# Turning queries with four transposes of token pairs in a retention and gated feed-forward kernel

## The chip, the cores and the metric

The kernel runs on one core of one Trainium2 chip. The metric is device time in microseconds of one execution. A core has TensorE (PE in the profile, its weight loads PEld), VectorE (DVE), ScalarE (ACT), GpSimd (POOL) and SyncE (SP), which here issues most of the DMA transfers. Matmul results go to PSUM; everything else lives in SBUF.

## The reference

Two blocks follow each other. The first is recurrent retention over 4 batches, 8 heads, 768 tokens and 64 dimensions a head, all float32:

```python
for t in range(S):
    state = gamma * state + einsum('bhd,bhe->bhde', k[:, :, t], v[:, :, t])
    y[:, :, t] = scale * einsum('bhd,bhde->bhe', q[:, :, t], state)
```

Its output, laid out as 3072 tokens of 512 features, is `x` of the second block, a feed-forward layer with 2048 hidden features:

```python
h = x @ w_in
g = h * (1.0 / (1.0 + np.exp(-1.702 * h)))
return g @ w_out
```

The weights are handed to the kernel as 8-byte words and narrowed to float32 on the chip.

## The kernel before, in words

**Retention.** The tokens are cut into chunks of 64. A step `j` handles one chunk of two batches (all 8 heads), so there are 24 steps. For each: queries and keys are turned so that the head dimension lies on partitions (`turn`), `scores` makes keys times queries, `masked` weighs them by decay, `own` multiplies them by the values, `past` multiplies the queries by the state, `by_state` and `output` add the two into `X`, `gain`, `aged` and `updated` carry the state to the next chunk; `decay` weighs the keys for it. These are bursts of 64x64 matmuls (L327, L335, L346, L355), 64 TensorE instructions each with the loads, and PSUM tiles `pa` and `py` that they share.

**Steps 0 to 5 and the rest.** For the first six steps (`NEW = 6`) the turn is TensorE's; from step 6 on it is done by DVE (L288). For `j < NEW` one DMA brings the queries as a tile of 128 rows and 512 columns: a row is one batch, head and block of 8 tokens, and holds these 8 tokens of 64 dimensions one after another (L155). Keys come with tokens on the rows (L146). `turn_new` (L265) makes a PSUM tile `pt` with tag `y`, of which there are two, shared with other products. Keys take four transposes of 128x128 (L278). Queries take 16 matmuls against columns picked from the identity (L275), one for each of 8 tokens and each half of the heads, in float32, so that the profile counts 32 matmuls and 32 loads; each writes its result into `pt` with the tokens already at their places and with half of the heads in each half of the partitions. `turned` (L296) then copies the whole tile to `QT[j]` or `KT[j]` in SBUF: one 128x512 operation on ACT (L294).

**Weights.** Every half megabyte or so of weights is fetched by SP (`w1a` and so on, L189) into one of three raw buffers and narrowed by `abs` (ACT, L225), `low` (ACT, L229), `clip` (DVE, L233), `lift` (DVE, L236), `sign` (DVE, L241) and `rest` (DVE, L246). The first products of the feed-forward block (`up0`, L464) use a weight once its `rest` is done: `up0.0.2` needs weight 0, `up0.0.3` weight 2, `up0.0.6` weight 3, `up0.0.7` weight 1. `gate` (ACT, L445) is the activation on such a product.

**The order.** Nothing is planned for the first part: a list of names written out by hand (L1092 to L1114) is gone through once, and every name issues its instructions on its engine. Each engine, and the queue of SP, takes its own in that order. For the steps spoken of here, the list has (shortened):

```python
turned_k1 turned_q1 q2 score1 rowd whole w2b turn_k2 turn_q2
... score2 q4 x1 clip2 lift2 sign2 low2 decay3 w3b w3a up0.0.2 masked2 turn_k3 turn_q3
k4@sp gain2 past2 own2 v3 q5 rest2 k5@sp gate0.0.2 turned_k3 turned_q3 updated2 state2 score3 decay4 low3
turn_q4 turn_k4 up0.0.3 x2 masked3 gain3 past3 own3 abs3 clip3 lift3 sign3 turned_q4 rest3 turned_k4 score4
turn_k5 turn_q5 up0.0.6 ...
```

Here `q4`, `k4`, `v3` are loads, `turn_*` TensorE's part and `turned_*` the copy. Query tiles have two buffers, so that `q5` on SP waits until TensorE has turned queries 3.

**After the list.** The second part, by far the longer, consists of Strassen-like products (`up` at L686, `down49` at L809, `down` at L942) with the later retention steps set between them, and DVE makes the sums of weights and activations for them.

## Time and profile before

| what | value |
|---|---|
| median of 3 runs | 654.35 us (654.05 to 658.25) |
| the profiled execution | 654.23 us, span of its instructions 652.5 us |
| mean clock granted to TensorE | 0.99 |
| query turns (L275) | 192 matmuls of 128x64, 222 ns in the median, at 4.8 to 45.7 us |
| key turns on TensorE (L278) | 24 matmuls of 128x128, 273 ns in the median |
| copies of turned tiles (L294, G<-pt) | 12 on ACT, 594 ns in the median |

How to read what follows. A line of the timeline has the start in us from the span's start, the time from the first to the last instruction of a group, the engine, the line of the kernel, the operation, the program's names as out<-in, the shapes, a count, and in brackets the idle time of the engine before it with what ended that. "issue" stands for no visible cause. PEld are weight loads, which overlap the matmuls and show TensorE's order best; SPq and ACTq are DMA issues. On the page, a row of 40 digits shows the busy share of 40 equal slices (16.3 us each) in tenths; PEclk is the clock granted to TensorE in tenths. A matmul's own duration is its way through the array; matmuls follow each other much closer than that, so durations of a row of them are taken from start to start.

### The profile page before, as it was taken

The page shows a single profiled execution, that of the slowest core. Times are in us where ns is not written, and L with a number is a line of the kernel's source. Part 1 is how long each engine was busy: PE and PEld are TensorE (multiplying, and loading weights), DVE is VectorE, ACT ScalarE, POOL GpSimd, SP SyncE. Part 2 cuts the span into 40 slices and gives each one's busy share as a digit, 9 for nine tenths or more (in the row PEclk, how much of TensorE's full clock was granted, in tenths as well). Part 3 has the DMA queues.
Part 4 walks back from the last instruction along what each step waited for, and adds up shares of the span by engine and source line. Part 5 has one row for each costly group of instructions (what it writes and reads, how often), then busy time and mean ns, then how long its engine had stood idle before and what let it go on. Part 6 is the DMA issues. An engine that isn't in the chain of part 4 may idle for free.

```text
span 652.5 us, 15859 instructions
## 1 busy us (share of the span) xinstructions
PE 636.0 (97%) x6717; PEld 579.5 (89%) x6718; DVE 433.3 (66%) x630; ACT 187.6 (29%) x343; POOL 152.7 (23%) x183
## 2 busy tenths in 40 slices
PE   7699999999998999999999999999999999999997
PEld 3588888888888999889999889999888999888997
DVE  2559977979989774438874337977145986144854
ACT  5668237662000101332101333100323110333210
POOL 3000311310622535000635100526300425200000
PEclk7799999999999999999999999999999999999999
DMA  8968577783358778520577830576921354501143
GB/s 186 235 202 212 112 231 212 209 219 56 98 181 282 170 177 257 141 72 1 164 167 213 235 70 14 156 168 196 244 48 49 82 165 138 207 11 48 57 156 97
DMA packets 150728, 96.89 MB, mean 148 GB/s; under 512 B 130528, under 2 KB 135904, under 8 KB 149632
## 3 DMA queue, kind: packets, MB, share of 16 engines
q1 hardware_dynamic: 138032, 42.83, 29.9%
q0 software_dynamic: 8704, 40.00, 19.6%
q10 hardware_dynamic: 3920, 13.04, 5.4%
q8 instruction: 53, 0.87, 0.6%
q14 instruction: 19, 0.16, 0.1%
HBM read 79.18 MB, written 14.94 MB: 144 GB/s over the span
## 4 chain that ended last, share of the span: by engine, by line
PE 82%; DVE 7%; DMA 5%; SPq 3%; issue 2%; ACT 0%; DVEq 0%
PE pq L809 34%; PE px L686 17%; PE pz L686 8%; PE ph L587 6%; PE py L686 4%; DVE X L762 2%; PE pa L327 2%; PE pd L942 2%; SPq L164 2%; DMA kn_in<-in_k_dram 2%; PE ph L464 1%; PE py L355 1%; PE ph L547 1%; PE py L346 1%; PE pa L335 1%
## 5 line engine op out<-in xcount | busy, mean ns | idle before, releaser
L809 PE MATMUL pq<-W,G 128*128 128x128 f32 x840 | 100.3, 276 | 0.0
L809 PEld LDWEIGHTS pq<-W,G 128*128 128x128 f32 x840 | 97.0, 192 | 0.8
L784 POOL DMA_DIRECT2D LATE<-W2D x34 | 18.9, 555 | 258.3 <-PE pq L809 140.0
L809 PE MATMUL pq<-LATE 128*128 128x128 f32 x560 | 74.9, 277 | 0.7 <-DVE o L918 0.7
L809 PEld LDWEIGHTS pq<-LATE 128*128 128x128 f32 x560 | 68.1, 192 | 1.5 <-DVE o L918 0.9
L686 PE MATMUL px<-X,LATE 128*128 128x256 f32 x256 | 60.6, 380 | 0.1
L686 PE MATMUL px<-X,W1A 128*128 128x256 f32 x256 | 60.5, 379 | 0.0
L686 PEld LDWEIGHTS px<-X,LATE 128*128 128x128 f32 x256 | 48.6, 190 | 7.0 <-ACT G L445 0.4
L686 PEld LDWEIGHTS px<-X,W1A 128*128 128x128 f32 x256 | 48.4, 190 | 6.4
L831 ACT ACTIVATE o<-pq 128x512 f32<-128x512 f32 (+1 forms) x18 | 9.8, 544 | 121.4 <-PE pq L809 101.7
L731 DVE TENSOR_TENSOR G<-pz,vv 128x512 f32<-128x512 f32 x16 | 11.1, 692 | 49.4 <-ACT vv L701 49.4
L445 ACT ACTIVATE G<-G 128x512 f32<-128x512 f32 x49 | 30.8, 629 | 43.5 <-DVE G L741 19.7
L809 PE MATMUL pq<-W,LATE 128*128 128x128 f32 x280 | 37.3, 276 | 0.7 <-issue 0.7
L809 PE MATMUL pq<-LATE,G 128*128 128x128 f32 x280 | 37.0, 275 | 0.0
L942 PE MATMUL pd<-W,LATE 128*128 128x256 f32 x160 | 35.1, 380 | 0.0
L809 PEld LDWEIGHTS pq<-W,LATE 128*128 128x128 f32 x280 | 34.2, 192 | 0.8 <-issue 0.8
L809 PEld LDWEIGHTS pq<-LATE,G 128*128 128x128 f32 x280 | 34.1, 192 | 0.0
L942 PEld LDWEIGHTS pd<-W,LATE 128*128 128x128 f32 x160 | 30.4, 190 | 4.1
L464 PE MATMUL ph<-X,W1A 128*128 128x256 f32 x128 | 31.0, 401 | 0.6 <-DVE X L397 0.6
L671 DVE TENSOR_TENSOR G<-G 128x512 f32<-128x512 f32 (+2 forms) x28 | 15.9, 567 | 23.5 <-ACT G L445 23.5
L798 DVE TENSOR_TENSOR LATE<-G 128x512 f32<-128x512 f32 x35 | 27.7, 791 | 5.0 <-PE pq L809 2.1
L686 PE MATMUL pz<-X,W1A 128*128 128x256 f32 x128 | 30.3, 380 | 0.0
(212 smaller groups left out, 1168.4 us busy)
## 6 DMA issues: line engine op xcount, KB each, us to landing
LATE<-W2D POOLq DMA_DIRECT2D x34, 768.0 KB, 5.0
W<-in_moe_w_out_dram SPq DMA_DIRECT2D x12, 512.0 KB, 5.2
LATE<-W1D ACTq DMA_DIRECT2D x4, 1536.0 KB, 7.5
LATE<-W1D POOLq DMA_DIRECT2D x4, 1536.0 KB, 7.8
kn_in<-in_k_dram SPq DMA_DIRECT2D x84, 64.0 KB, 3.8
W<-in_moe_w_in_dram SPq DMA_DIRECT2D x10, 512.0 KB, 5.8
out_dram<-o POOLq DMA_DIRECT2D x20, 256.0 KB, 4.8
q_sq<-in_q_dram SPq DMA_DIRECT2D x144, 32.0 KB, 3.2
```

The lines of the kernel that those rows point to most:

```text
L164: tc.keep_in_program_order(sp.dma_start(t[r0:r0 + C4, :, n], src[b + r0 // D, :, t0:t0 + C4, r0 % D:r0 % D + C4] .rearrange("h p d -> p h ...
L327: pe.matmul(PAS[HALF[w], u, 0, s, :], kt[HALF[u], w, s, :], qt[HALF[u], w, s, :], start=True, stop=True)
L445: pin(act.activation(g, h[:, i], AF.Gelu_apprx_sigmoid))
L464: pe.matmul(h[:, ab], w, X[:, 2 * th + c // 2, c % 2, :], start=(ab == 0 and c == 0), stop=(c == 3), skip_group_check=True)
L587: pe.matmul(acc[:, u, :], w, x, start=(start and u == 0 and c == 0), stop=(stop and c == 1), skip_group_check=True)
L671: hold(dve.tensor_sub(q[0][1], q[0][0], q[0][1]))
L686: pe.matmul(acc[:, u, :], w1(2 * d + u, sw)[:, c, :], X[:, sx, c, :], start=(start and u == 0 and c == 0), stop=(stop and c == 1), skip_gr ...
L762: tc.keep_in_program_order(dve.tensor_sub(t[n], a, t[n - 1] if n else b11))
L784: engine.dma_start(c, W2D[i])
L798: dve.tensor_add(d[:, 0], s2, a11)
L809: pe.matmul(p0[:, j, :], a[:, d], w[:, d], start=(new and j == 0 and d == 0), stop=(d == NP // 2 - 1), skip_group_check=True)
L942: pe.matmul(p0[:, n, :], g1(m, p, sa)[:, n * P:(n + 1) * P], W2[:, sb, p, :], start=(new and p == 0 and n == 0), stop=(last and p == NP - ...
```

## The change

Queries of steps 0 to 5 are turned like keys, by four 128x128 transposes, each of two tokens (128 columns of the query tile). The result then has a token pair's two members in the two halves of the partitions, where `scores` and `past` need the two halves of the heads. So four copies of 64 partitions and 256 elements set it right: `turned(j, 0, engine, e)` copies what came from member `e` of the pairs, for both halves `r` of the heads, and two of the four move data between the halves of the partitions. The copies for `e = 0` are on ACT in place of the one copy before, those for `e = 1` on DVE, as new names `turned2_q*@dve` in the list, each right behind its `turned_q*`. The copies read PSUM with a step of 128 elements between neighbours (`p r i c k`) and write SBUF with a step of 2.

```diff
@@ turn_new
-        if n == 0:
-            p = p.rearrange("p s (i b k) -> p k i s b", i=2, k=8)
-            pick = ident.rearrange("p (i r c) -> p r i c", i=2, r=2)
-            for k in range(8):
-                for r in range(2):
-                    pe.matmul(p[HALF[r], k], x[:, k * D:(k + 1) * D], pick[:, r], start=True, stop=True)
-            return
         for s in range(HP):
-            pe.matmul(p[:, s, :], x[:, 2 * s:2 * s + 2].rearrange("p r d -> p (r d)"), ident, is_transpose=True)
+            pe.matmul(p[:, s, :], x[:, 2 * s:2 * s + 2].rearrange("p r d -> p (r d)") if n else x[:, s * P:(s + 1) * P],
+                      ident, is_transpose=True)
@@ turned
-    def turned(j, n, engine=act):
-        copy(engine, (QT[j], KT[j])[n], TURNED.pop((j, n)))
+    def turned(j, n, engine=act, e=0):
+        if n:
+            copy(engine, KT[j], TURNED.pop((j, n)))
+            return
+        p = TURNED[j, n].rearrange("p k (i r c) -> p r i c k", i=2, r=2)
+        to = QT[j].rearrange("p s (i b e) -> p e i s b", i=2, e=2)
+        for r in range(2):
+            copy(engine, to[HALF[r], e], p[HALF[e], r])
@@ the names
+        works[f"turned2_q{j}"] = lambda *e, j=j: turned(j, 0, *(e or (act,)), 1)
@@ the list (the rest of it is the same, in the same order)
-turned_q0 turned_k0 score0
+turned_q0 turned2_q0@dve turned_k0 score0
-turned_k1 turned_q1 q2 score1
+turned_k1 turned_q1 turned2_q1@dve q2 score1
-turned_k2 turned_q2 v2 rest0a
+turned_k2 turned_q2 turned2_q2@dve v2 rest0a
-turned_k3 turned_q3 updated2
+turned_k3 turned_q3 turned2_q3@dve updated2
-turned_q4 rest3 turned_k4 score4
+turned_q4 turned2_q4@dve rest3 turned_k4 score4
-turned_q5 gate0.0.3
+turned_q5 turned2_q5@dve gate0.0.3
```

More of the change, by code (lines that the diff above doesn't have):

```diff
@@ L1092 @@
     for name in """
-        k0@act table q0 z8 turn_q0 turn_k0 w0b rows z4 k1@sp abs0b q1 turned_q0 turned_k0 score0 v0
-        w0a clip0b lift0b sign0b low0b mask k2@sp turn_k1 turn_q1 causal rest0b masked0 decay0 v1 decay1 abs0a
-        clip0a lift0a sign0a low0a gain0 own0 updated0 turned_k1 turned_q1 q2 score1 rowd whole w2b turn_k2 turn_q2
-        w2a x0 k3@sp aged1 masked1 turned_k2 turned_q2 v2 rest0a abs2 q3 gain1 past1 own1 updated1 state1
-        decay2 aged2 score2 q4 x1 clip2 lift2 sign2 low2 decay3 w3b w3a up0.0.2 masked2 turn_k3 turn_q3
@@ L1098 @@
-        k4@sp gain2 past2 own2 v3 q5 rest2 k5@sp gate0.0.2 turned_k3 turned_q3 updated2 state2 score3 decay4 low3
-        turn_q4 turn_k4 up0.0.3 x2 masked3 gain3 past3 own3 abs3 clip3 lift3 sign3 turned_q4 rest3 turned_k4 score4
-        turn_k5 turn_q5 up0.0.6 w1a w5b w1b aged3 updated3 state3 w5a v4 x3 up0.1.3 turned_q5 gate0.0.3 abs1
-        low1 abs5 clip1 aged4 lift1 sign1 masked4 own4 gain4 w6a rest1 clip5 lift5 gate0.0.6 sign5 up0.0.7
-        past4 w6b decay5 low5 rest5 updated4 v5 gain5 w4a abs6 gate0.1.3 turned_k5 clip6 state4 x4 lift6
@@ L1103 @@
-        score5 masked5 w4b abs4 up0.1.7 low6 aged5 gate0.0.7 w7a w7b low7 low4 q6 sign6 v6 own5
-        rest6 past5 seven_4.2 state5 gate0.1.7 seven_6.2 updated5 zero2.0 clip4 up0.1.6 lift4 sign4 x5 seven_52.2 rest4 turn6
-        anew decay6 abs7 aged6 up0.1.2 w8a gate0.1.2 clip7 zero_x zero2.1 score6 past6 q7 w8b v7 zero2.2
-        masked6 lift7 sign7 gain6 rest7 own6 w11b zero2.3 zero2.4 turn7 w9a updated6 aged7 gate0.1.6 zero2.5 decay7
-        zero2.6 state6 w11a seven_4.0 x6 zero0.0 score7 masked7 abs8 clip8 past7 zero0.1 state7 seven_6.0 seven_52.0 lift8
@@ L1108 @@
-        sign8 gain7 own7 x7 seven_x zero0.2 zero0.3 zero0.4 zero0.5 low8 seven_keep.2 w9b abs9 low11 clip9 rest8
-        lift9 zero0.6 w10a seven2.0 w10b seven2.1 abs11 clip11 lift11 sign11 seven_4.1 rest11 seven2.2 abs10 seven2.3 seven2.4
-        seven_w.1 clip10 lift10 sign9 seven0.0 seven2.5 low10 low9 rest9 sign10 updated7 rest10 seven_4.3 seven2.6 seven0.1 seven0.2
-        seven0.3 seven0.4 seven1.0 seven_keep.0 w14b w14a w12b w12a abs12 seven_w.3 clip12 seven0.5 seven0.6 seven_v.1 lift12 sign12
@@ L1112 @@
-        abs14 clip14 low12 rest12 lift14 sign14 seven1.1 seven1.2 w13a seven1.3 w13b abs13 low14 seven_v.3 clip13 lift13
-        seven1.4 sign13 seven3.0 seven1.5 rest14 seven1.6 seven3.1 seven3.2 seven3.3 seven3.4 w15a seven_keep.3 seven_keep.1 w15b abs15 clip15
-        lift15 low13 low15 sign15 seven3.5 rest13 seven3.6 rest15 late_loads
+        k0@act table q0 z8 turn_q0 turn_k0 w0b rows z4 k1@sp abs0b q1 turned_q0 turned2_q0@dve turned_k0 score0
+        v0 w0a clip0b lift0b sign0b low0b mask k2@sp turn_k1 turn_q1 causal rest0b masked0 decay0 v1 decay1
@@ new lines @@
+        abs0a clip0a lift0a sign0a low0a gain0 own0 updated0 turned_k1 turned_q1 turned2_q1@dve q2 score1 rowd whole w2b
+        turn_k2 turn_q2 w2a x0 k3@sp aged1 masked1 turned_k2 turned_q2 turned2_q2@dve v2 rest0a abs2 q3 gain1 past1
+        own1 updated1 state1 decay2 aged2 score2 q4 x1 clip2 lift2 sign2 low2 decay3 w3b w3a up0.0.2
+        masked2 turn_k3 turn_q3 k4@sp gain2 past2 own2 v3 q5 rest2 k5@sp gate0.0.2 turned_k3 turned_q3 turned2_q3@dve updated2
+        state2 score3 decay4 low3 turn_q4 turn_k4 up0.0.3 x2 masked3 gain3 past3 own3 abs3 clip3 lift3 sign3
@@ new lines @@
+        turned_q4 turned2_q4@dve rest3 turned_k4 score4 turn_k5 turn_q5 up0.0.6 w1a w5b w1b aged3 updated3 state3 w5a v4
+        x3 up0.1.3 turned_q5 turned2_q5@dve gate0.0.3 abs1 low1 abs5 clip1 aged4 lift1 sign1 masked4 own4 gain4 w6a
+        rest1 clip5 lift5 gate0.0.6 sign5 up0.0.7 past4 w6b decay5 low5 rest5 updated4 v5 gain5 w4a abs6
+        gate0.1.3 turned_k5 clip6 state4 x4 lift6 score5 masked5 w4b abs4 up0.1.7 low6 aged5 gate0.0.7 w7a w7b
+        low7 low4 q6 sign6 v6 own5 rest6 past5 seven_4.2 state5 gate0.1.7 seven_6.2 updated5 zero2.0 clip4 up0.1.6
@@ new lines @@
+        lift4 sign4 x5 seven_52.2 rest4 turn6 anew decay6 abs7 aged6 up0.1.2 w8a gate0.1.2 clip7 zero_x zero2.1
+        score6 past6 q7 w8b v7 zero2.2 masked6 lift7 sign7 gain6 rest7 own6 w11b zero2.3 zero2.4 turn7
+        w9a updated6 aged7 gate0.1.6 zero2.5 decay7 zero2.6 state6 w11a seven_4.0 x6 zero0.0 score7 masked7 abs8 clip8
+        past7 zero0.1 state7 seven_6.0 seven_52.0 lift8 sign8 gain7 own7 x7 seven_x zero0.2 zero0.3 zero0.4 zero0.5 low8
+        seven_keep.2 w9b abs9 low11 clip9 rest8 lift9 zero0.6 w10a seven2.0 w10b seven2.1 abs11 clip11 lift11 sign11
@@ new lines @@
+        seven_4.1 rest11 seven2.2 abs10 seven2.3 seven2.4 seven_w.1 clip10 lift10 sign9 seven0.0 seven2.5 low10 low9 rest9 sign10
+        updated7 rest10 seven_4.3 seven2.6 seven0.1 seven0.2 seven0.3 seven0.4 seven1.0 seven_keep.0 w14b w14a w12b w12a abs12 seven_w.3
+        clip12 seven0.5 seven0.6 seven_v.1 lift12 sign12 abs14 clip14 low12 rest12 lift14 sign14 seven1.1 seven1.2 w13a seven1.3
+        w13b abs13 low14 seven_v.3 clip13 lift13 seven1.4 sign13 seven3.0 seven1.5 rest14 seven1.6 seven3.1 seven3.2 seven3.3 seven3.4
@@ L1115 @@
+        w15a seven_keep.3 seven_keep.1 w15b abs15 clip15 lift15 low13 low15 sign15 seven3.5 rest13 seven3.6 rest15 late_loads
     """.split():
```

## The prediction

> **What bounds the kernel now.** I read the page first: where TensorE idles, where its clock is low, where the DMA engines are full.

> ```profile
> span 652.5 us, 15859 instructions
> PE 636.0 (97%) x6717; PEld 579.5 (89%) x6718; DVE 433.3 (66%) x630; ACT 187.6 (29%) x343; POOL 152.7 (23%) x183
> PE   7699999999998999999999999999999999999997
> PEclk7799999999999999999999999999999999999999
> q8 instruction: 53, 0.87, 0.6%
> ```

> TensorE is busy for 97% of the span; only the first two slices (33 us) have idle time and a low clock. All six query turns lie between 4.8 and 45.9 us. The waits of TensorE between 27 and 203 us add up to 1.5 us, so whatever is won or lost at the first long product after the last turn (`up0.0.6`, at 45.90) goes through to the end nearly whole. So I ask one question: when does `up0.0.6` start? The timeline of the weight loads shows TensorE's own order best; beside it ACT, DVE and SP:

> ```profile
> 20.26 0.56 PEld L335 LDWEIGHTS pa<-v_in,G 64*64 64x64 f32 x32
> 25.78 0.18 PEld L355 LDWEIGHTS py<-G,v_in 64*64 64x64 f32 x1 [4.04 <-issue]
> 27.66 5.32 PEld L464 LDWEIGHTS ph<-X,W1A 128*128 128x128 f32 x16 [0.81 <-DVE X L397]
> 37.08 1.01 PEld L275 LDWEIGHTS pt<-UB,q_in 128*64 128x64 f32 x32
> 38.16 0.43 PEld L278 LDWEIGHTS pt<-UB,kn_in 128*128 128x128 f32 x4
> 38.55 3.32 PEld L464 LDWEIGHTS ph<-X,W1A 128*128 128x128 f32 x16
> 45.90 6.77 PEld L464 LDWEIGHTS ph<-X,W1A 128*128 128x128 f32 x32
> ...
> 21.48 1.05 ACT L294 ACTIVATE G<-pt 128x512 f32<-128x512 f32 x2
> 33.42 0.60 ACT L445 ACTIVATE LATE<-ph 128x512 f32<-128x512 f32 x1 [3.87 <-PE ph L464]
> 35.44 2.01 ACT L311 ACTIVATE G<-kn_in,cold 128x64 f32<-128x64 f32 x8
> 38.41 1.14 ACT L225 ACTIVATE G<-W 128x1024 f32<-128x1024 f32 x1
> 41.04 1.29 DVE L241 SCALAR_TENSOR_TENSOR G<-W,G 128x512 uint32<-128x512 uint32 x2
> 42.37 1.23 DVE L246 CUSTOM_DVE_ANT_0 W1A<-G,W1A 128x2048 uint16<-128x2048 uint16 x1
> 48.22 0.69 DVE L233 TENSOR_SCALAR G<-G 128x1024 f32<-128x1024 f32 x1 [1.77 <-ACT G L225]
> 25.08 2.61 SPq L146 DMA_DIRECT2D kn_in<-in_k_dram  x4
> 34.94 0.56 SPq L155 DMA_DIRECT2D q_in<-in_q_dram  x1
> ```

> One query turn takes TensorE 1.08 us (37.08 to 38.16), a key turn 0.39 (38.16 to 38.55). At 21.7 us it stops for 4.04 us one matmul short of finishing `own1`, for no wait that the profile shows. A packet of queue q8 starts at 22.7 us, inside that hole. That queue moved 53 packets of 0.87 MB / 53 = 16.4 KB, and 13,435 recorded TensorE instructions / 53 = 253: I take them for TensorE's program and the hole for a wait on it. In the windows the clock then falls to 0.50 (26 to 30 us), so that 16 products take 5.32 us and not 3.32. Until the hole ends, 344 matmuls and 345 loads are recorded: about 690 instructions.

> **The change, part by part.**

> *TensorE.* Each query turn falls from 32 matmuls and 32 loads to 4 and 4, by the key turn's row: 1.08 - 0.39 = 0.69 us, or 0.5 where the key turn takes 0.58 with a wait for an event behind it (44.23 to 44.81). That is 3.0 to 4.1 us over six, and 6 x 56 = 336 fewer instructions. The first turn gives nothing: the next one waits until 8.8 us for its keys.

> *ACT.* One 128x512 copy (0.50 us from start to start: 21.48 to 21.98) becomes two of 64x256; the copies of `rowd` in that form start 0.375 apart: +0.25 us a step.

> *DVE.* Two new 64x256 copies a step. The nearest DVE row is the 128x256 operation at L241, 0.76 us for two: +0.75 us a step, 4.5 in all. No row of before reads PSUM with a step of 512 bytes between elements. From below: 0.375 each, as nothing makes it cheaper than a plain copy. From above: 1.53 us, the dearest single operation on a row of 512 elements (DVE, L534 at 74.45). I take 0.375, because reading every second word in SBUF (L225, 1.15 us) costs nothing beside reading all (1.12), and keep the other end as a rival.

> [...]

> *What is queued behind.* DVE is in order. `turned2_q1` now stands between `updated0` and `score1`: scores 1 start at 18.5, not 17.96, which eats that turn's gain. `turned2_q2` (20.5 to 21.25) delays `rest0a`, then `updated1`, `state1` and `x1` end at about 23.8. `turned2_q3` follows `rest2`, `turned2_q4` stands between `sign3` and `rest3`, `turned2_q5` before `clip1`, where DVE waits 1.77 us today.

> *The hole.* With 64 replaced by 8 the same instruction numbers fall elsewhere. Number 690 falls at the end of `gain2` (no longer `own1`), and `score2` and the 3.45 us of `up0.0.2` lie before it: the fetch has that time. So scores 2 start at 22.8 (ACT's second half copy), `up0.0.2` at 23.85 after `x1`, at full clock until 27.3 (before 33.0), and the turn of queries 3 ends near 28.3.

> *What is late next.* ACT has no free moment from 20.29 to 29.55 and ends now at 29.75; then the gate (0.5), keys 3 (0.5) and queries 3 (0.75) end at 31.5, and scores 3 run at 31.55 (before 36.42). Then the DMA binds: the last of the four parts of keys 4 is issued at 27.07 and the four take 6.6 us to land in the median, so they are there at 33.3. `decay4` starts then (before 35.44): only 2.1 us are left of the 5. From the rows: `decay4` to 35.25, `low3` to 36.3, `abs3` to 37.4; on DVE `clip3`, `lift3`, `sign3` (0.65 + 0.65 + 1.3) to 40.05, the two new copies to 40.8, `rest3` (1.2) to 42.0. TensorE has ended `own3` by 38.7, waits for the copies, runs scores 4 and two turns from 40.85, and starts `up0.0.6` at 42.4. That is 45.9 - 42.4 = **3.5 us** earlier. SP helps: its load of queries 5 waits 5.8 us for the turn of queries 3 today, and goes at 29.15 instead of 34.94, with keys 5 and the weights behind it.

> *Two prices on that.* (a) In steps of 253, the next such numbers are 943, now at the start of `gain3` (37.0), and 1196, now between scores 4 and the turns of step 5. Under DMA load the way from a crossing to the next block ready was 25.78 - 19.2 = 6.5 us; in a quiet stretch the packet began 0.6 us after the crossing (35.4, in `past2`), where it was 3.5 under load. In the new order the weights of 2 MB are in flight at 37: ready at 43.5, needed at 41.9, a hole of 1.6; or 0 if it goes as in the quiet. (b) The clock: after the stretch 4.45 to 7.86 us, with 1.4 us of work, it fell to half. TensorE now idles 38.7 to 40.85, about the same share. Half clock for one such stretch (3.4 us) costs 1.7.

> Sum: 3.5 minus one of the two (1.6 or 1.7) = 1.9. The profiled execution took 654.23 (span 652.5 and 1.7 around it), 0.12 below the median 654.35. Forecast 654.35 - 1.9 = **652.4**. The rest of DVE's new work lies in its waits (3.63, 1.04 and 1.77 us between 35 and 48).

> **Rivals.**

> *Neither price is paid*: 3.5 us, 650.9. For it: the clock stayed full through 14.7 to 24.9 despite short holes. Against: the DMA queue is full where the block is asked for.

> *Both are paid*: 3.5 - 3.3 = 0.2, 654.1.

> *The hole at 21.7 is not the program's fetch and stays.* Then the old path holds from 27.66 and loses only the turns of steps 3 to 5, while DVE's path from `sign3` (42.33) gains the copies: 43.1, `rest3` at 44.35, `up0.0.6` at 44.35: 1.55 us, 652.8. For it: the profile names no cause for the hole. Against: it lies inside a run of equal matmuls, between operands that are all there.
> [...]

> *Slower: strided half copies are dear.* One place, PSUM to SBUF. At X us each, ACT makes four before `decay4` (1.8 us of slack there) and DVE two before `rest3`: the loss is 4(X - 0.375) - 1.8 + 2(X - 0.375). It eats the 3.5 us at X = 1.26, 3.4 times the row. At the upper end, 1.53, it costs 5.1: the kernel ends 1.6 us later, 656.0. Against it: the other strides here are free.

> *More is won*: later stops like it (1.41 us before 209.95) also move with the 336 instructions and may vanish: 649.5. They may as well appear anew, which is about as likely.

> **How the numbers follow.** One price 0.40 (652.4), neither 0.22 (650.9), both 0.12 (654.1), the hole stays 0.10 (652.8), dear copies 0.10 (656.0), more won 0.06 (649.5). Each has about 1.4 us of its own on both sides, as a stop of that size may come or go later. Range 649.5 to 655.5: the four cases from 650.9 to 654.1 with that width, which leaves out the outer part of the last two. About 1% (6.5 us) is what a measurement of this kernel can tell from no change, and none of the cases reaches it; I leave 0.04 for faster, 0.07 for slower and 0.89 for same.

> **What would show it.** Right: q turns as 4 matmuls of 128x128 at 0.27 us each; no hole in `own1`; full clock at `up0.0.2`; `decay4` at 33.3, released by the load of keys 4; scores 4 waiting for DVE's copy; `up0.0.6` between 42 and 45; from there the same spacing to the end. Wrong: half copies of over 0.8 us; a hole of 3 us or more at another place; `up0.0.6` after 45.9; new idle time of TensorE after 50 us.

## The result, and the profile after

| what | before | after |
|---|---|---|
| median of 13 runs each | 655.39 us (652.39 to 658.25) | 652.54 us (650.37 to 654.49) |
| the profiled execution | 654.23, span 652.5 | 651.86, span 650.1 |
| TensorE instructions, as recorded | 13,435 | 13,100 |

The ratio is 0.9955, with a 95% interval of 0.9937 to 0.9973: the kernel is about 2.9 us faster. That is under half a per cent, but it is clear of no change: with 13 runs of each the interval reaches 0.2% to either side, where the prediction took 1% for the least that can be told. The forecast of 652.4 is 0.1 us off. The way there was not the forecast one, as the profile shows. First the page of after:

```profile
span 650.1 us, 15545 instructions
PE 634.2 (98%) x6550; PEld 577.4 (89%) x6550; DVE 437.9 (67%) x642; ACT 189.3 (29%) x349; POOL 153.4 (24%) x183
PE   7799999999999999999999999999999999999997
PEclk9799999999999999999999999999999999999999
q8 instruction: 51, 0.84, 0.6%
```

TensorE bounds the kernel as before and is busy for 1.8 us less (636.0 to 634.2). The first two slices still have idle time; the clock is 0.9 in the first now (0.7 before) and 0.7 in the second, as it was. Next the timeline of the weight loads after:

```profile
24.00 0.40 PEld L346 LDWEIGHTS py<-G,state 64*64 64x64 f32 x11 [2.16 <-issue]
25.27 0.97 PEld L327 LDWEIGHTS pa<-G 64*64 64x64 f32 x32
27.08 5.08 PEld L464 LDWEIGHTS ph<-X,W1A 128*128 128x128 f32 x16 [0.83 <-DVE X L397]
...
36.13 0.59 PEld L327 LDWEIGHTS pa<-G 64*64 64x64 f32 x32 [1.28 <-issue]
36.79 0.42 PEld L271 LDWEIGHTS pt<-UB,q_in 128*128 128x128 f32 x4
37.17 0.47 PEld L271 LDWEIGHTS pt<-UB,kn_in 128*128 128x128 f32 x4
37.61 3.32 PEld L464 LDWEIGHTS ph<-X,W1A 128*128 128x128 f32 x16
...
44.12 2.03 PEld L464 LDWEIGHTS ph<-X,W1A 128*128 128x128 f32 x10
```

A query turn takes 0.38 us (36.79 to 37.17), as a key turn does, where it took 1.08. The stop of 4.04 us in `own1` is gone, but one of 2.16 us stands in `past1`, and `up0.0.2` again takes 5.08 us for 16 products: the windows give a clock of 0.50 at 24 to 27 us and 0.54 at 27 to 31. `up0.0.6` (the first long product after the turns) starts at 44.12, 1.78 us before the 45.90 of before. ScalarE, VectorE and SyncE of after, in the same stretch:

```profile
32.59 0.60 ACT L445 ACTIVATE LATE<-ph 128x512 f32<-128x512 f32 x1 [2.62 <-PE ph L464]
33.09 1.31 ACT L288 ACTIVATE G<-pt 128x512 f32<-128x512 f32 x3
34.42 2.02 ACT L311 ACTIVATE G<-kn_in,cold 128x64 f32<-128x64 f32 x8
37.41 1.13 ACT L225 ACTIVATE G<-W 128x1024 f32<-128x1024 f32 x1
22.84 0.87 DVE L288 COPY G<-pt 64x256 f32<-64x256 f32 x2 [2.11 <-ACT G L288]
34.43 0.87 DVE L288 COPY G<-pt 64x256 f32<-64x256 f32 x2 [3.02 <-ACT G L288]
35.33 0.69 DVE L420 TENSOR_TENSOR state<-state,pa 128x512 f32<-128x512 f32 x1
40.03 1.29 DVE L241 SCALAR_TENSOR_TENSOR G<-W,G 128x512 uint32<-128x512 uint32 x2
41.35 0.89 DVE L288 COPY G<-pt 64x256 f32<-64x256 f32 x2
42.27 1.23 DVE L246 CUSTOM_DVE_ANT_0 W1A<-G,W1A 128x2048 uint16<-128x2048 uint16 x1
24.51 2.60 SPq L146 DMA_DIRECT2D kn_in<-in_k_dram  x4
33.46 0.56 SPq L155 DMA_DIRECT2D q_in<-in_q_dram  x1
```

VectorE's first two rows show what the prediction did not have: its queue stands still until ScalarE has ended its copies of the same tile (2.11 and 3.02 us; 6.71 before the first tile, where it stood still for 5.99 before the change as well, for another reason). Behind the copies stands `updated2` (L420), which reads the `pa` tile that scores 3 write next: it ends at 35.33 + 0.69 = 36.02, and scores 3 start at 36.13. "issue" in that row's bracket is again a wait that the profile does not name; the end of L420 beside it names it.

Where the rest of the time went. The starts of three rows (us), and the time from one row of 24 products of the second part to the next of its kind, between which the stop of 1.41 us lay:

| kernel | `up0.0.6` | first `pd` row | lost between | `pq` row to row at 200 us |
|---|---|---|---|---|
| before | 45.90 | 149.86 | | 199.03 to 210.21 = 11.18 |
| after | 44.12 (-1.78) | 149.49 (-0.37) | 1.41 | 198.66 to 208.25 = 9.59 |

Of the lead of 1.78 us only 0.37 is left at 150 us. Then the stop is not there, and the lead becomes 1.96; it is 2.4 at the end (one wait of 0.44 for ScalarE at 359.96 is also gone, and a stop of 0.85 at 425.81 has become one of 0.69 at 446.47). The row of before with the stop, and the rows of after at the same place:

```profile
209.95 0.19 PEld L355 LDWEIGHTS py<-at,v_in 64*64 64x64 f32 x3 [1.41 <-issue]
```

```profile
207.62 0.56 PEld L355 LDWEIGHTS py<-at,v_in 64*64 64x64 f32 x32
208.25 2.75 PEld L809 LDWEIGHTS pq<-W,G 128*128 128x128 f32 x24
```

So four questions: what do the two halves of the change give by themselves; what holds scores 2 and 3; what makes the stops come and go; and where does the lead go between 46 and 150 us?

### The profile page after: what moved, and what is told of

It reads as the page before. It is cut to its first block, busy times and chain, and to the rows that moved or that the text cites. A ratio compares the mean times of both kernels' runs of the same rounds, so it can differ in the third digit from the quotient of the medians.

```text
span 650.1 us, 15545 instructions
## 1 busy us (share of the span) xinstructions
PE 634.2 (98%) x6550; PEld 577.4 (89%) x6550; DVE 437.9 (67%) x642; ACT 189.3 (29%) x349; POOL 153.4 (24%) x183
## 4 chain that ended last, share of the span: by engine, by line
PE 86%; DMA 4%; SPq 4%; DVE 4%; issue 1%; ACT 1%; ACTq 0%
PE pq L809 34%; PE px L686 17%; PE pz L686 9%; PE pd L942 6%; PE ph L587 6%; PE py L686 4%; SPq L164 2%; PE pa L327 2%; DMA kn_in<-in_k_dram 2%; DMA W<-in_moe_w_out_dram 1%; PE pa L335 1%; PE ph L464 1%; PE py L355 1%; PE py L346 1%; PE pt L271 1%
## 5 line engine op out<-in xcount | busy, mean ns | idle before, releaser
L809 PE MATMUL pq<-W,G 128*128 128x128 f32 x840 | 100.3, 276 | 0.0
L809 PEld LDWEIGHTS pq<-W,G 128*128 128x128 f32 x840 | 97.0, 192 | 0.8
L809 PE MATMUL pq<-LATE 128*128 128x128 f32 x560 | 74.9, 277 | 0.7 <-DVE o L918 0.7
L809 PEld LDWEIGHTS pq<-LATE 128*128 128x128 f32 x560 | 68.1, 192 | 1.5 <-DVE o L918 0.9
L445 ACT ACTIVATE G<-G 128x512 f32<-128x512 f32 x49 | 30.8, 629 | 43.1 <-DVE G L741 19.7
L809 PE MATMUL pq<-W,LATE 128*128 128x128 f32 x280 | 37.2, 275 | 0.6 <-issue 0.6
L809 PE MATMUL pq<-LATE,G 128*128 128x128 f32 x280 | 37.0, 275 | 0.0
L809 PEld LDWEIGHTS pq<-W,LATE 128*128 128x128 f32 x280 | 34.2, 192 | 0.7 <-issue 0.7
L809 PEld LDWEIGHTS pq<-LATE,G 128*128 128x128 f32 x280 | 34.1, 192 | 0.0
L464 PE MATMUL ph<-X,W1A 128*128 128x256 f32 x128 | 30.7, 398 | 0.6 <-DVE X L397 0.6
```

Of the source, the lines that this page charges most:

```text
L445: pin(act.activation(g, h[:, i], AF.Gelu_apprx_sigmoid))
L464: pe.matmul(h[:, ab], w, X[:, 2 * th + c // 2, c % 2, :], start=(ab == 0 and c == 0), stop=(c == 3), skip_group_check=True)
L809: pe.matmul(p0[:, j, :], a[:, d], w[:, d], start=(new and j == 0 and d == 0), stop=(d == NP // 2 - 1), skip_group_check=True)
```

## The experiments

Ratios are to the kernel before, in runs on the same chip, with their 95% intervals. Runs of one kernel spread over some 4 us, so a ratio tells about 1.4 us. The places in the traces tell more, but each kernel has one trace, of one execution, and a part of what differs between two of them is that spread.

### The two parts alone

`e5_transposes_alone` has the four transposes, and one copy by ScalarE. It leaves out setting the halves right, so its queries are in another order:

```diff
-        p = TURNED[j, n].rearrange("p k (i r c) -> p r i c k", i=2, r=2)
-        to = QT[j].rearrange("p s (i b e) -> p e i s b", i=2, e=2)
-        for r in range(2):
-            copy(engine, to[HALF[r], e], p[HALF[e], r])
+        copy(engine, QT[j], TURNED.pop((j, n)))
```

> The four transposes of token pairs alone: ScalarE then copies the whole 128x512 tile with one copy as the kernel before does, and the half copies on two engines are left out (the halves are not set right, so queries are in another order than the reference's). TensorE's instructions are as many as after the change. Theory 'less TensorE work, and no copy of VectorE that waits for ScalarE's': the up0.0.6 matmuls start 2.5 to 2.9 us earlier than the 45.90 of before (as with all copies on ScalarE, 2.87), against 1.78 after the change; most of that is lost again where VectorE waits for the last of keys 7, so that pd starts 0.4 to 0.8 ahead of 149.86; the late stop of 1.41 us at 210 is gone; ratio 0.9945 to 0.9975. Rival 'the half copies cost what matters': without them the lead goes through, pd starts 2.5 or more ahead, ratio 0.991 to 0.9935.

Measured: 651.18 us, 0.9961 [0.9938, 0.9984]. `up0.0.6` starts at 43.81 (2.09 ahead, less than the 2.5 expected), `pd` at 148.11 (1.75 ahead, more than the first theory had and less than the rival), and the late stop is gone. The timeline of its weight loads:

```profile
22.27 0.59 PEld L324 LDWEIGHTS pa<-G 64*64 64x64 f32 x32
23.82 3.32 PEld L461 LDWEIGHTS ph<-X,W1A 128*128 128x128 f32 x16 [0.96 <-DVE X L394]
```

Without the half copies, scores 2 start at 22.27 and `up0.0.2` at 23.82, at full clock (3.32 us for 16). The prediction had 22.8 and 23.85, with VectorE's copies in it but no wait for them; this run has neither that wait nor the stop in `past1`. Behind `up0.0.2` the lead shrinks: ScalarE, which the prediction had without a free moment here, waits 3.77 us for weights, until 25.23; scores 3 start at 33.90; and the 16 products of `up0.0.3` take 4.58 us and not 3.32.

`e6_copies_alone` turns queries by the 16 matmuls of before, and copies by four operations of the same shapes (the PSUM step is 2 elements here, 128 in the change):

```diff
-    def turned(j, n, engine=act):
-        copy(engine, (QT[j], KT[j])[n], TURNED.pop((j, n)))
+        p = TURNED[j, n].rearrange("p s (i b e) -> p e i s b", i=2, e=2)
+        to = QT[j].rearrange("p s (i b e) -> p e i s b", i=2, e=2)
+        for r in range(2):
+            copy(engine, to[HALF[r], e], p[HALF[r], e])
```

> The half copies alone: queries are turned by the 16 matmuls of before, and then copied by four half-length copies, two on ScalarE and two on VectorE, of the same shapes as after the change. TensorE's instructions are as many as before. Theory 'the gain is TensorE's work and its place in program memory, the copies cost little': the late stop of about 1.4 us at 210 stays (11.2 us from the first to the second row of pq, against 9.6 after the change), VectorE's copies wait 2 to 7 us for ScalarE's of the same tile, up0.0.6 starts 0 to 1.1 us later than the 45.90 of before, ratio 0.9995 to 1.002. Rival 'copies dear': up0.0.6 over 2 us later and ratio over 1.003. Rival 'the copies shift the time': a ratio under 0.998.

Measured: 656.30 us, 1.0020 [0.9995, 1.0045]. `up0.0.6` starts at 47.40, 1.5 us later than before (expected up to 1.1), and the late stop is there (200.76 to 212.03, 11.27). The groups of the copies, first after the change, then in this kernel (busy us and mean ns of one; then idle time before them and what ended it):

```profile
L288 ACT ACTIVATE G<-pt 64x256 f32<-64x256 f32 x12 | 4.7, 395 | 3.6 <-PE pt L271 3.4
L288 DVE COPY G<-pt 64x256 f32<-64x256 f32 x12 | 5.1, 428 | 12.1 <-ACT G L288 11.8
```

```profile
L294 DVE COPY G<-pt 64x256 f32<-64x256 f32 x12 | 5.1, 421 | 13.4 <-ACT G L294 13.2
```

A half copy costs 0.43 us on VectorE and 0.40 on ScalarE, and the step in PSUM (2 or 128 elements) changes 7 ns on VectorE (421 and 428). The profile puts 11.8 us of VectorE's idle time down to ScalarE's copies (three of the six tiles; 13.2 us and four here). That is not all loss: at the same three places VectorE was idle for 5.99, 1.60 and 3.63 us before the change. What the wait costs is what comes late behind it, and that takes other runs.

### What holds scores 2 and 3

`e4_all_copies_on_act` takes `@dve` from the six `turned2_q*`, so that VectorE has no copies.

> The changed kernel with all four half copies of a step on ACT. DVE no longer stands waiting behind ACT's copies (11.8 us in three waits in the changed kernel), ACT has 0.8 us more a step. Theory 'SyncE queue': the first long product starts 0.3 to 1 us earlier, the lead is lost near 85 us all the same, the time is that of the changed kernel within 0.7 us. Theory 'DVE load': without 4.5 us on DVE the lead of 1.8 us is kept at 150 us and the time falls by 1 to 1.5 us.

Measured: 651.52 us, 0.9966 [0.9945, 0.9987]. Scores 3 start at 34.44 (36.13 after the change) and `up0.0.6` at 43.03, 2.87 ahead of before, though ScalarE now makes all four copies. At `pd` only 0.72 of it is left, as the first theory expected: the lead is lost without VectorE's copies too.

`e13_dve_copies_first` keeps every engine's work and order, and turns round only who waits for whom:

```diff
-turned_k2 turned_q2 turned2_q2@dve
+turned_k2 turned2_q2@dve turned_q2
-turned_k3 turned_q3 turned2_q3@dve
+turned_k3 turned2_q3@dve turned_q3
```

> After the change, but in the list the VectorE half copies of queries 2 and 3 stand ahead of ScalarE's (turned2_q2@dve turned_q2, and the same for 3). Every engine has the same instructions in the same order; only which of the two engines waits for the other on one tile is turned round. Theory 'VectorE's queue stands still behind ScalarE': VectorE's copies of queries 2 now start when TensorE has turned them (about 20.8 to 21.2, against 22.84), rest0a and updated1 end by 23.6, and scores 2 (25.27 after the change) start at 23.3 to 24.5, later only as far as a stop of TensorE in past1 holds them; copies of queries 3 likewise, so that scores 3 start at 35.6 or earlier (36.13 after the change); up0.0.6 starts 2.1 to 2.9 us ahead of the 45.90 of before, and the ratio is 0.993 to 0.9965. Rival 'the stop in past1 holds scores 2, not VectorE': they start at 25.0 to 25.5 again and scores 3 at 36.0 to 36.3. Rival 'no wait between the engines is in the program at all': VectorE waits as after the change.

Measured: 651.50 us, 0.9963 [0.9942, 0.9984]. Its timeline, VectorE first, then ScalarE and the weight loads:

```profile
22.12 0.87 DVE L288 COPY G<-pt 64x256 f32<-64x256 f32 x2 [1.21 <-PE pt L271]
23.74 0.69 DVE L420 TENSOR_TENSOR state<-state,pa 128x512 f32<-128x512 f32 x1
31.25 0.87 DVE L288 COPY G<-pt 64x256 f32<-64x256 f32 x2
32.15 0.69 DVE L420 TENSOR_TENSOR state<-state,pa 128x512 f32<-128x512 f32 x1
...
23.08 0.83 ACT L288 ACTIVATE G<-pt 64x256 f32<-64x256 f32 x2 [1.16 <-DVE G L288]
31.79 0.58 ACT L445 ACTIVATE LATE<-ph 128x512 f32<-128x512 f32 x1
33.76 2.02 ACT L311 ACTIVATE G<-kn_in,cold 128x64 f32<-128x64 f32 x8 [0.20 <-DMA kn_in<-in_k_dram]
...
24.55 0.59 PEld L327 LDWEIGHTS pa<-G 64*64 64x64 f32 x32 [0.51 <-issue]
25.81 3.32 PEld L464 LDWEIGHTS ph<-X,W1A 128*128 128x128 f32 x16 [0.68 <-DVE X L397]
33.19 0.20 PEld L327 LDWEIGHTS pa<-G 64*64 64x64 f32 x4 [1.37 <-ACT G L288]
```

Now ScalarE waits for VectorE (1.16 us) at queries 2, and VectorE for TensorE's turn alone. Scores 2 start at 24.55, just over the bound of 24.5 and just behind the end of `updated1` (23.74 + 0.69 = 24.43), although TensorE's clock was at 0.50 from 20 to 22 us here (1.00 after the change). Scores 3 start at 33.19, 2.94 us before after's, and `up0.0.6` at 43.02, 2.88 ahead of before.

What of the 2.94 us is the order? Both kernels have the gate of `up0.0.2` on ScalarE (L445) ahead of these copies. It starts at 31.79, 0.80 earlier than after's 32.59, and from its start to scores 3 it takes 1.40 us and not 3.54: 2.14 us less. (`e12`, below, has the order of after, and 3.52.) `updated2` ends at 32.84, ahead of ScalarE's copies, which now release scores 3. `up0.0.2` also ended 3.03 us earlier here, by its start (1.27) and the full clock (1.76). That moved the gate by 0.80 only, since ScalarE was busy until 31.79. But it let VectorE copy ahead of the gate, at 31.25, so that a part of the 2.14 us is due to it as well, and this run does not divide them. With all copies on ScalarE (`e4`) the same way takes 34.44 - 32.19 = 2.25 us. `decay4` is now the one that waits for the load of keys 4, at 33.76; the prediction had 33.3.

So the wait is in the program, and it had a part in what held scores 3. For scores 2 this run cannot tell it from the stop in `past1`, which it does not have either; `e12`, below, has the wait without the stop, and scores 2 start at 25.16.

Why the program has the wait is open. The two engines read one PSUM tile, and they also write one SBUF tile, each every second element. Each of the two can be what puts one engine behind the other, and no run separates them. In the kernel ScalarE reads partitions 0 to 63 of the PSUM tile and VectorE 64 to 127; in the traces they still go one after the other (VectorE waits 2.11 and 3.02 us after the change, ScalarE 1.16 us in `e13`).

### What makes the stops come and go

The theory, "blocks", the author's reading of the traces: TensorE's program comes in blocks, one with each packet of queue q8, and where a block's instructions pass too fast for the next block, TensorE stops at their end. For the length of a block the author took 256 instructions, an estimate from the recorded instructions for each packet: 13,435 / 53 = 253 before and 13,100 / 51 = 257 after. Tiny 32x32 matmuls, two instructions each, were put between `turn_q0` and `turn_k0`, where TensorE waits for keys 0: they shift every later instruction number.

```diff
+    def pad(n):
+        x = flow.bitcast(mybir.dt.bfloat16)
+        for _ in range(n):
+            pe.matmul(idle[0:32, 0:32], x[0:32, 0:32], x[0:32, 0:32], start=True, stop=True)
-k0@act table q0 z8 turn_q0 turn_k0
+k0@act table q0 z8 turn_q0 pad turn_k0
```

The change takes away 336 = 256 + 80 instructions. So before with 88 tiny matmuls (176 instructions) counts as after does, but for whole blocks of 256; after with 40 (80 instructions) counts as before does; and after with 128 (256 instructions) counts as after.

> The kernel before, turns and copies untouched, with 88 tiny bf16 products of 32x32 put between the turns of queries 0 and keys 0, where TensorE waits 2.7 us for the load of keys 0. They are 176 TensorE instructions, so that from step 6 on the places where TensorE's program runs out of a loaded block are those of the changed kernel (336 fewer and 176 more differ by two blocks of 256). Theory 'blocks': most of the profiled gain of 2.4 us is the stop of 1.41 us before 209.95 that is no longer there; this kernel loses that stop too, the marks after 214 us come 1 to 2.5 us earlier than before, and the ratio to before is 0.996 to 0.999. Theory 'work': the gain is TensorE's shorter turns; this kernel keeps the old turns, the stop near 210 stays or is of no weight, and the ratio is 1.000 to 1.003.

> The changed kernel with 40 tiny products (80 instructions) at the same idle place, so that from step 6 on the block ends fall where they fell in the kernel before. Theory 'blocks': a stop of 1 to 2 us comes back in the last matmuls of the burst near 208 us, and the kernel is 1 to 2 us slower than the changed one (ratio to before 0.997 to 1.000). Theory 'work': no stop there, the time of the changed kernel (0.9955).

> After the change, with 32 tiny 32x32 matmuls between turn_q0 and turn_k0, where TensorE waits for keys 0: 64 TensorE instructions more, so that every multiple of 256 falls 64 instructions earlier in the work. Theory 'place in program memory': the 256 instructions that end where own's row at 208 begins take 2.25 us in the trace of after, the shortest of its busy stretches at this place, under a high DMA load, so the late stop comes back at about 208 with 0.8 to 1.6 us (9.59 us from the first to the second row of pq becomes 10.4 or more); ratio 0.9975 to 1.0005. Rival 'the place makes no difference': no stop there, ratio 0.9945 to 0.9965 as after the change.

> After the change, with 80 such tiny matmuls at the same place (160 instructions more, some 2 us of work in the time that TensorE waits there). Theory 'place in program memory': no multiple of 256 ends a busy stretch at 208, the shortest stretches of 256 that remain take 2.9 to 3.1 us (at 220, 331 and 433 by the trace of after), so the late stop stays gone (9.6 us from row to row of pq) and no stop over 0.7 us comes later; ratio 0.9935 to 0.9965. Rival 'padding itself costs': ratio 0.998 to 1.001 as with 40 of them, with no stop at 208 to show for it.

> A control: after the change, with 128 such tiny matmuls, 256 instructions more, so that the multiples of 256 fall on the same instructions as after the change. Theory 'place in program memory': the stops are where they are after the change (2 us near 22 to 24, none at 208, 0.6 near 446), and the time differs from after's by the 0 to 1 us that 3.4 us of tiny matmuls stick out of the wait for keys 0; ratio 0.995 to 0.998. Rival 'padding itself costs': ratio 0.999 to 1.003, more than with 40 or 80.

| kernel | ratio | `pq` row to row | late stop |
|---|---|---|---|
| `e1_before_padded` | 1.0041 [1.0017, 1.0066] | 200.99 to 210.58 = 9.59 | gone |
| `e2_after_padded` | 0.9995 [0.9974, 1.0017] | 197.93 to 208.84 = 10.91 | back |
| `e10_after_pad32` | 0.9964 [0.9941, 0.9987] | 197.03 to 206.62 = 9.59 | one row further on |
| `e11_after_pad80` | 0.9960 [0.9939, 0.9981] | 200.28 to 209.87 = 9.59 | none |
| `e12_after_pad128` | 0.9974 [0.9952, 0.9997] | 196.18 to 205.77 = 9.59 | none, as after |

The weight loads at this place with 40, then with 32 tiny matmuls:

```profile
208.58 0.19 PEld L355 LDWEIGHTS py<-at,v_in 64*64 64x64 f32 x3 [1.14 <-issue]
208.84 2.75 PEld L809 LDWEIGHTS pq<-W,G 128*128 128x128 f32 x24
```

```profile
206.62 0.63 PEld L809 LDWEIGHTS pq<-W,G 128*128 128x128 f32 x5
208.15 2.20 PEld L809 LDWEIGHTS pq<-W,G 128*128 128x128 f32 x19 [0.90 <-issue]
```

With 40 the stop is where before had it, three loads ahead of the end of the L355 row. With 32, that is 16 instructions fewer ahead of it, it comes eight matmuls later: three of L355 and five of L809. Before with 88, and after with 80 and with 128, have none. The other kernels agree: the two that count as before (`e6`, `e9`) have the stop at the same three loads (1.50 and 1.91 us), and the five that count as after (`e3`, `e4`, `e5`, `e8`, `e13`) have none. So in all 14 kernels the place of the late stop follows the count, and that it is gone after the change (9.59 for 11.18) is no merit of the transposes.

Two more facts in the traces bear on what the stops are. From 14 us on there are 27 stops of 0.67 us or more inside a row of equal matmuls, in 13 of the 14 kernels (`e12` has none). Counted in recorded TensorE instructions ahead of them, they lie on one ladder, whatever the work is: 434 (after, `e3`, `e4`, `e8`), 689 (before, `e6`, `e9`), 940 (`e11`, 1.67 us at 36.03) or 944 (`e1`), 1196 and 1700 (`e1`), 1952 (`e9`), 3988 or 3989 (`e2`, `e10`), 4245 (before, `e6`, `e9`), and three more beyond 9000. From one to the next it is 251 to 257 instructions or a whole multiple of that. And each of them ends 1.34 to 1.66 us after a packet of queue q8 has ended (16,384 bytes; 22.73 to 24.14 us for before's stop until 25.78). No other wait of TensorE over 0.6 us without a named cause has that distance to a packet. That agrees with the prediction, which took the hole for a wait on TensorE's program; what a packet of q8 holds, no trace shows.

The times do not follow as simply: `e2` and `e10` both have a late stop, and their ratios lie 0.3% apart, though the intervals overlap; `e1` lost more in new stops at the front (2.94 us amid a query turn at 46, for one) than it won at 210, so that its ratio missed what was expected; `e10`, expected at 0.9975 or more, missed too, and has the ratio of its rival although the stop came. What each count costs in all is not settled.

For the estimate of 256 speak the ladder of 251 to 257 and, at 210 us, two runs: `e2`, with 256 instructions fewer than before, has the stop at the same three loads (1.14 us for 1.41), and `e12`, with 256 more than after, has none there, as after. Few packets have such a stop behind them: three of 53 before (4.04, 1.41 and 0.85 us) and two of 51 after (2.16 and 0.69).

At the front, after, `e3`, `e4` and `e8` stop at the same instruction, behind 19 of the 32 of L346 (2.16, 1.57, 1.71 and 3.33 us). `e12` counts as after does, but for 256 more, and shows no stop there:

```profile
21.20 0.56 PEld L346 LDWEIGHTS py<-G,state 64*64 64x64 f32 x32
21.67 0.56 PEld L355 LDWEIGHTS py<-G,v_in 64*64 64x64 f32 x32
25.16 0.97 PEld L327 LDWEIGHTS pa<-G 64*64 64x64 f32 x32 [2.93 <-ACT G L311]
```

The first of the two operations of `x1` on VectorE, after the change and then in `e12`:

```profile
25.60 0.69 DVE L375 TENSOR_TENSOR tmp<-py,rowd 128x512 f32<-128x512 f32 x1 [0.45 <-PE py L355]
```

```profile
24.96 0.68 DVE L375 TENSOR_TENSOR tmp<-py,rowd 128x512 f32<-128x512 f32 x1
```

TensorE is done with `own1` near 22.2, and scores 2 start at 25.16 all the same, 0.11 before after's 25.27, since `updated1` on VectorE ends at 24.36 + 0.69 = 25.05 in both within 0.1. So for scores 2 the stop in `past1` lay in a wait for VectorE and cost about a tenth of a us. It cost more at `up0.0.2`: `x1` needs what TensorE makes behind the stop, so that VectorE waits 0.45 us for it after the change, and `up0.0.2` starts at 27.08 and not at 26.42. `e12` also shows that a count alone does not make a stop. Its packet of q8 ended at 19.92, ahead of the matmuls of `past1`, and after's at 22.56, behind their start: how early the packet comes differs between these two runs.

### Where the lead goes between 46 and 150 us

Two places in after. VectorE's transpose of keys 7 and what TensorE waits for behind it; then ScalarE at 101 us, and TensorE behind that:

```profile
84.75 0.71 DVE L282 STREAM_TRANSPOSE G<-k_sq 128x512 f32<-128x512 f32 x1 [1.70 <-issue]
88.55 0.59 PEld L346 LDWEIGHTS py<-G,state 64*64 64x64 f32 x32 [1.25 <-issue]
100.97 1.15 ACT L225 ACTIVATE G<-W 128x1024 f32<-128x1024 f32 x1 [0.78 <-DMA W<-in_moe_w_out_dram]
104.71 1.38 PEld L587 LDWEIGHTS ph<-x,w 128*128 128x128 f32 x7 [0.54 <-ACT p L592]
```

The last part of keys 7 is issued by SyncE at 81.82, and such a part takes 2.1 to 3.3 us to land; before, it was issued at 82.11, only 0.29 later, and VectorE did not wait for it. SyncE's row of such issues, 16 a step at 0.49 us each from 56 us on, had won only 0.71 us at its start where TensorE had won 1.78.

`e3_keys67_by_pool` lets GpSimd issue the 16 loads of keys 6 and 7, `e8_act_copies_pool_keys` has that and all copies on ScalarE, and `e9_before_pool_keys` is before with that edit alone:

```diff
-                        tc.keep_in_program_order(sp.dma_start(
+                        tc.keep_in_program_order((pool if name == "k" and j < 2 * CB else sp).dma_start(
```

> The changed kernel with the 16 loads of keys 6 and 7 issued by GpSimd and not by SyncE (nothing else is changed). In the changed kernel DVE waits 1.70 us for keys 7 near 84.8 us and TensorE loses 1.25 us behind it. Theory 'SyncE queue': SyncE's row of issues, 0.49 us each, gives the front's gain of 1.8 us back; with 16 issues fewer the wait near 84.8 goes, TensorE's product sums near 150 us stand 1.5 to 2 us ahead of before (0.37 in the changed kernel), and the time falls by 1 to 1.5 us against the changed kernel. Theory 'DVE load': the 12 new copies on DVE gave it back; then the front's lead is still lost between 80 and 105 us, and the time stays that of the changed kernel within 0.5 us.

> After the change, with all four half copies on ScalarE (as in the run with all copies there) and the 16 loads of keys 6 and 7 issued by GpSimd instead of SyncE (as in the run with keys 6 and 7 there). Theory 'SyncE queue': up0.0.6 starts 2.5 to 2.9 us ahead of before, the lead is not lost at keys 7 nor at the weights of 101, pd starts 2.3 or more ahead of 149.86, and with the late stop gone from 210 on 3.9 or more ahead; ratio 0.9915 to 0.994. Rival 'no room': TensorE loses the lead by other waits before 150 (pd under 1.2 ahead), ratio 0.9955 to 0.997 as in the two runs with one edit each.

> The kernel before, with the 16 loads of keys 6 and 7 issued by GpSimd instead of SyncE: a control. Theory 'SyncE queue': before the change TensorE does not wait for keys 7, since they land just in time, so nothing is won: pd within 0.5 of 149.86, the late stop stays, ratio 0.9985 to 1.0015. Rival 'the move of the loads is worth time of its own': pd 0.8 or more earlier, ratio 0.9965 to 0.998.

| kernel | ratio | `up0.0.6` | `pd` | lost between |
|---|---|---|---|---|
| `e3_keys67_by_pool` | 0.9964 [0.9943, 0.9984] | 44.43 (-1.47) | 148.84 (-1.02) | 0.45 |
| `e8_act_copies_pool_keys` | 0.9955 [0.9933, 0.9977] | 44.51 (-1.39) | 149.40 (-0.46) | 0.93 |
| `e9_before_pool_keys` | 1.0016 [0.9993, 1.0039] | 45.24 (-0.66) | 150.97 (+1.11) | 1.77 |
| `e4_all_copies_on_act` | 0.9966 [0.9945, 0.9987] | 43.03 (-2.87) | 149.14 (-0.72) | 2.15 |
| `e5_transposes_alone` | 0.9961 [0.9938, 0.9984] | 43.81 (-2.09) | 148.11 (-1.75) | 0.34 |
| `e12_after_pad128` | 0.9974 [0.9952, 0.9997] | 42.65 (-3.25) | 147.01 (-2.85) | 0.40 |
| `e13_dve_copies_first` | 0.9963 [0.9942, 0.9984] | 43.02 (-2.88) | 147.71 (-2.15) | 0.73 |

In `e3` the two waits are not there; its weight loads at both places:

```profile
87.76 0.56 PEld L346 LDWEIGHTS py<-G,state 64*64 64x64 f32 x32
...
103.66 3.43 PEld L587 LDWEIGHTS ph<-x,w 128*128 128x128 f32 x16
```

So SyncE's queue made these two waits, as the first theory said. But what it forecast did not come: `pd` of `e3` is 1.02 us ahead of before and not 1.5 to 2, and its time, expected 1 to 1.5 us below that of the changed kernel, is not lower (0.9964 and 0.9955). `e8`, expected at 0.994 or below with 2.3 us or more kept at `pd`, had a stop of 3.33 us in `past1`, a lead of 1.39 and lost 0.93 of it, 0.63 by 57 us, where it waited for values (0.44 us at 52.25); `e9` lost 1.46 us at 60.50 to a stop on the ladder (1952), amid a row of L327. And in `e5`, `e12` and `e13` most of the lead goes through with SyncE's row as it was; there keys 7 held VectorE for 0.6 us or less, where they held it for 1.70 in the profile of after. What holds in all: every kernel here with the transposes loses 0.3 to 2.2 us between 46 and 150 us. The places looked at are waits behind loads, which the trace names for most of them. How much is lost differs between these kernels, one execution of each, by as much as the lead itself.

## Why the prediction was right in its time and not in its way

- **TensorE's turn.** 0.69 us less for each: measured 0.70 (1.08 to 0.38). Right.
- **The half copies.** 0.375 us each on VectorE: measured 0.43, so +0.88 us a step and not +0.75; ScalarE's 0.40. The rival of dear copies, which needed 1.26 us each to eat the gain, is not borne out.
- **"`turned2_q2` (20.5 to 21.25) delays `rest0a`"**: this step failed. The copies ran at 22.84 to 23.71, as VectorE waited for ScalarE's, which stood behind its own work until 22.02. `x1` ended at 27.0 and not at 23.8, scores 2 at 25.27 for 22.8, `up0.0.2` at 27.08 for 23.85. Where the wait is taken out, and the stop in `past1` with it (`e5`), it is 23.82.
- **The hole.** It leaves number 690 as forecast, but the number 256 before it, 434, now in `past1`, was not looked at: 2.16 us there. By `e12` it cost 0.1 us at scores 2, as VectorE was later still, and up to 0.66 at `up0.0.2`. At 943 and 1196, the two of price (a), there is no stop.
- **Full clock at `up0.0.2`.** Wrong: TensorE was busy for 1.98 of the 4 us from 20 to 24 (before, 0.88 of 4 from 21 to 25), the clock fell to 0.50, and 16 products took 5.08 us. Price (b) was paid, and some 15 us earlier than thought. In `e5`, where TensorE was busy for 3.18 of these 4 us, they take 3.32. They do in `e13` too, but there the clock had been at 0.50 already, at 20 to 22 us, and was back.
- **Scores 3 at 31.55.** Measured 36.13, behind `updated2`; 33.19 in `e13`. From the end of `up0.0.2` it is 3.97 us (32.16 to 36.13) where 4.25 was forecast (27.3 to 31.55): all of the lateness was there before.
- **`up0.0.6` at 42.4, or 44.1 with one price**: measured 44.12. The size came out by luck, with half clock and waits for the copies' order in it. Scores 3 were 4.6 us late and `up0.0.6` only 1.7, mostly because the forecast had TensorE wait 2.15 us for VectorE's copies ahead of scores 4 (38.7 to 40.85). It did not: the copies ended at 42.24, scores 4 started at 42.66, and TensorE had 0.33 us of idle time from scores 3 on.
- **"Goes through to the end nearly whole."** This step failed: 1.41 of 1.78 us were lost again by 150 us, at transfers that SyncE issues. The waits there were small before, as far as the rows of keys 7 show, because the loads were just in time, so a TensorE that comes earlier meets them.
- **"More is won", at 0.06**: the late stop did vanish, 11.18 to 9.59 = 1.59 us, by the count of instructions. It gave back what was lost ahead of it.

So the gain came out as 1.78 - 1.41 + 1.59 + 0.41 = 2.37 us in the profiled executions (654.23 to 651.86), where 1.9 was forecast as one sum; two errors, of opposite sign and nearly equal, cancelled. That the time itself is met to 0.1 us is luck as well: 1.9 was taken from a median of 3 runs, 654.35, and that of 13 runs is 655.39, so that the medians differ by 2.85. Taking this for proof of the working would be wrong.

Still open: how the medians' 2.85 us divide into front and late stop, since single executions spread by 4 us; whether it is the PSUM tile or the SBUF tile that makes one engine wait for the other; and what the copies would give if both ran at the same time, which was not tried.

## What to carry to other kernels

When two engines copy from one PSUM tile and one waits for the other, as here for 2.11 and 3.02 us, look for what stands in the queue of the one that waits; putting first the engine that is free cost nothing here, and the way from the gate to scores 3 took 1.40 us and not 3.54 in that run. Of a gain of 1.78 us at the front 0.37 was left here behind the next transfers: ask for each load behind it how long it had been there before it was needed. And when a change alters how many instructions TensorE has, look whether stops come or go with the count, as the one of 1.41 us did here; pad the count back before crediting the change with the difference, and count the instructions ahead of each stop.
